# FFT and routed experts on one core: the first two half batches in a hand-written order, with the early loads on two queues

## Chip, core and metric

One core of a Trainium2 chip runs the whole kernel. The metric is the device time of one execution in microseconds (us), and the kernel before takes 1115.26 us, the median of three runs.

## What is computed

```python
X = np.fft.fft(np.fft.fft(x, axis=1), axis=2).real      # x: 8 x 2496 x 256
x = X.reshape(19968, 256)
logits = x @ w_gate                                     # 8 experts
expert_idx = np.argmax(logits, axis=1)
probs = softmax(logits); gate_w = probs[rows, expert_idx]
for e in range(8):
    mask = expert_idx == e
    h = np.maximum(x[mask] @ w1[e], 0.0)                # F = 1024
    out[mask] = gate_w[mask, None] * (h @ w2[e])
```

## The kernel before

The real part of the two transforms is folded by symmetry, so that each of the 8 batches becomes two half batches (even and odd). I number these 0 to 15: half batch 2b + par is the half `par` of batch b. A batch of x (2.6 MB) is loaded in five column slots; the first batch comes in three pieces, slots 0 and 1 (A), 2 and 3 (B), and 4 (C).

**Per half batch.** DVE folds the batch in place (`fold_w` L403, `fold_fg` L408 and L410, `fold_z` L418, `fold_h` L429 and L431). TensorE runs the *S stage* along the sequence (`s_mm` L319, matmuls L321), twice (q0, q1), and ACT and DVE evict each (`s_stage` L343, L348 to L353). The *D stage* (`along_d` L559, matmuls L567 and L568) makes five column tiles; for each ACT does three copies (L570 to L572) and DVE two (L573, L574). `route_a` (L461) makes the logits (L466), an exponent on ACT (L475), a one-hot (L483) and its bf16 copy on ACT (L487). `route_b` (L498) counts the tokens of each expert by two small matmuls (L503, L504) and a scan (L509), makes each token's slot (`di`, L521), and POOL scatters the rows into buckets in DRAM, ten scatters for a half batch (L525).

**Expert part.** After half batches 1, 3, 6, 10 and 15 a *group table* is made on DVE (`group_table` L639, `table_row` L688); its row goes to SP by DMA (L695), and SP's registers then give the addresses of the rows and weights of the groups that follow. `moe_steps` (L881) loads weights (`load_w`, L757) and rows (`load_rows`, L727), transposes on TensorE (L773), splits into a high and a low part for fp32 accuracy (ACT L775, L788, L799; DVE L776, L789, L800) and multiplies (L813 to L815, L845 to L856). Two groups belong to the first table, ten to the second.

**What sets the order.** Both parts are generators of steps; the scheduler of the language puts the instructions on the engines in an order of its own, within constraints given in the code (`issue_after`). Each engine works its list in order. Nearly all loads are on SP's DMA queue; batch 1 and the token ids (`load_rest` L256) are on POOL's. A bulk of dummy matmuls (`spin` L312, `WARM = 16, 40`) runs before the first fold is ready and while folds run. `fold_first` (L446) folds batch 0, `fold_batch` (L437) the others; `pads` (L540) writes the ends of the buckets; `load_x` (L223) loads a later batch into the buffer of the one two before. `gate_weights` (L379), `g1_fold` (L358), `g1_sums` (L367), `g1_rows` (L372) and `gate_g1` (L389) do a column that stands apart and its share of the logits. POOL also makes a bf16 copy of a triangle for the router (`trib`, L309) and puts the ids into the rows (`put_ids` L457).

## Time and profile before

| what | value |
|---|---|
| runs | 1114.73, 1115.26, 1116.75 us; median 1115.26 |
| profiled execution | 1110.62 us, span of its trace 1108.5 |
| granted clock of TensorE, mean | 0.989 |
| busy: TensorE / DVE / ACT / POOL | 97% / 74% / 54% / 33% of the span |
| bytes moved | 183.13 MB, 165 GB/s on average |

The profile is of one execution and its times are from the start of the span; 2.1 us of the 1110.62 lie around it. An engine's idle time matters only where work that ends the kernel waits for it. The trace names what ended each wait, by semaphores.

### The profile page before, as it was taken

The page shows a single profiled execution, that of the slowest core. Times are in us where ns is not written, and L with a number is a line of the kernel's source. Part 1 is how long each engine was busy: PE and PEld are TensorE (multiplying, and loading weights), DVE is VectorE, ACT ScalarE, POOL GpSimd, SP SyncE. Part 2 cuts the span into 40 slices and gives each one's busy share as a digit, 9 for nine tenths or more (in the row PEclk, how much of TensorE's full clock was granted, in tenths as well). Part 3 has the DMA queues.
Part 4 walks back from the last instruction along what each step waited for, and adds up shares of the span by engine and source line. Part 5 has one row for each costly group of instructions (what it writes and reads, how often), then busy time and mean ns, then how long its engine had stood idle before and what let it go on. Part 6 is the DMA issues. An engine that isn't in the chain of part 4 may idle for free.

```text
span 1108.5 us, 20006 instructions
## 1 busy us (share of the span) xinstructions
...
## 2 busy tenths in 40 slices
...
GB/s 352 162 197 243 141 316 196 232 238 253 231 183 82 274 202 145 138 163 144 153 190 133 151 127 156 134 159 120 157 132 161 122 54 72 149 200 46 40 68 194
DMA packets 175761, 183.13 MB, mean 165 GB/s; under 512 B 146107, under 2 KB 147037, under 8 KB 162978
## 3 DMA queue, kind: packets, MB, share of 16 engines
...
q0 software_dynamic: 16352, 45.10, 11.2%
...
## 4 chain that ended last, share of the span: by engine, by line
PE 85%; issue 6%; DMA 3%; DVE 2%; POOL 2%; ACT 1%; SPq 0%; POOLq 0%; DVEq 0%; ACTq 0%
PE psY L855 21%; PE psH L815 13%; PE psH L814 13%; PE psH L813 13%; PE psY L856 11%; PE psH L321 5%; PE psY L845 2%; PE psY L848 2%; PE psY L847 2%; PE psH L567 1%; PE psH L568 1%; DMA pack<-c_pack 1%; DMA x<-xin 1%; POOL out L869 1%; PE psH L773 1%
## 5 line engine op out<-in xcount | busy, mean ns | idle before, releaser
L855 PE MATMUL psY<-wb,hh 128*128 128x512 f32 x1104 | 401.7, 397 | 1.2 <-DVE ohf L483 0.9
L869 POOL DMA_INDIRECT out<-ys,gt x162 | 175.0, 1080 | 530.4 <-DVE ys L868 448.1
L856 PE MATMUL psY<-wb,hl 128*128 128x256 f32 x1104 | 309.0, 280 | 0.0
L813 PE MATMUL psH<-xh,wah 128*128 128x512 f32 (+1 forms) x832 | 291.0, 350 | 0.7 <-ACT xh L775 0.7
L815 PE MATMUL psH<-xh,wal 128*128 128x512 f32 (+1 forms) x832 | 288.0, 346 | 0.0
L814 PE MATMUL psH<-xl,wah 128*128 128x512 f32 (+1 forms) x832 | 287.8, 346 | 0.0
L819 DVE SCALAR_TENSOR_TENSOR hl<-psH,hh 128x512 fp32r<-128x512 f32 x324 | 222.0, 685 | 39.4 <-ACT hh L818 36.2
L855 PEld LDWEIGHTS psY<-wb,hh 128*128 128x128 f32 x1104 | 207.3, 188 | 52.5 <-issue 5.5
L789 DVE TENSOR_TENSOR wal<-w1r,wah 128x512 fp32r<-128x512 f32 x208 | 143.2, 689 | 141.9 <-ACT wah L788 141.3
L788 ACT CAST wah<-w1r 128x512 fp32r<-128x512 f32 x208 | 129.1, 621 | 203.7 <-PE psH L814 198.6
L818 ACT ACTIVATE hh<-psH 128x512 fp32r<-128x512 f32 x324 | 192.9, 595 | 53.7 <-PE psH L815 53.5
L525 POOL DMA_INDIRECT bucket<-rb,di x160 | 175.3, 1096 | 129.6 <-issue 78.5
L856 PEld LDWEIGHTS psY<-wb,hl 128*128 128x128 f32 x1104 | 208.2, 189 | 9.0
L813 PEld LDWEIGHTS psH<-xh,wah 128*128 128x128 f32 x832 | 157.6, 189 | 25.3 <-issue 3.0
L815 PEld LDWEIGHTS psH<-xh,wal 128*128 128x128 f32 x832 | 157.8, 190 | 19.1
L799 ACT CAST wb<-w2r 128x512 fp32r<-128x512 f32 x208 | 129.9, 624 | 73.1 <-PE psY L856 55.7
L800 DVE TENSOR_TENSOR wb<-w2r,wb 128x512 fp32r<-128x512 f32 x208 | 142.8, 686 | 35.0 <-ACT wb L799 34.7
L814 PEld LDWEIGHTS psH<-xl,wah 128*128 128x128 f32 x832 | 158.1, 190 | 10.7
L775 ACT CAST xh<-psH 128x512 fp32r<-128x512 f32 x81 | 47.5, 587 | 47.3 <-DVE psH L769 44.7
L866 ACT ACTIVATE ys<-psY,gt 128x256 f32<-128x256 f32 x162 | 66.0, 479 | 7.7 <-PE psY L848 4.6
L776 DVE TENSOR_TENSOR xl<-psH,xh 128x512 fp32r<-128x512 f32 x81 | 55.6, 687 | 17.7 <-ACT xh L775 16.1
L321 PE MATMUL psH<-cs,x 64*128 64x313 f32 (+3 forms) x280 | 66.1, 439 | 0.0
...
## 6 DMA issues: line engine op xcount, KB each, us to landing
...
```

Of the source, the lines that this page charges most:

```text
L525: ins = nc.gpsimd.indirect_dma_start(out=bucket[:, :], out_offset=IndirectOffsetOnAxis(ap=di[:, n : n + 1].bitcast(U32), axis=0), in_=rb[: ...
L789: nc.vector.tensor_sub(lo, src, hi.bitcast(F32))
L799: nc.scalar.copy(wb[:, :, 0], src)
L800: nc.vector.tensor_sub(wb[:, :, 1], src, wb[:, :, 0].bitcast(F32))
L813: nc.tensor.matmul(o, lhsT=wh[:, c], rhs=xh[:, k, :], start=(k == 0), stop=False)
L814: nc.tensor.matmul(o, lhsT=wh[:, c], rhs=xl[:, k, :], start=False, stop=False)
L815: nc.tensor.matmul(o, lhsT=wl[:, c], rhs=xh[:, k, :], start=False, stop=(k == 1))
L818: nc.scalar.activation(hh, hp, AF.Relu)
L819: nc.vector.scalar_tensor_tensor(out=hl, in0=hp, scalar=0.0, in1=hh.bitcast(F32), op0=ALU.max, op1=ALU.subtract)
L855: nc.tensor.matmul(y, lhsT=hh[:, c], rhs=wide_w, start=(first and q == 0), stop=end, skip_group_check=True)
L856: nc.tensor.matmul(y[:, 0:D], lhsT=hl[:, c], rhs=wb[:, f, 0], start=False, stop=end, skip_group_check=True)
L869: ins = nc.gpsimd.indirect_dma_start(out=out, out_offset=IndirectOffsetOnAxis(ap=gt[:, a, 1:2].bitcast(U32), axis=0), in_=ys, in_offset=No ...
```

## The change

- The early loads go to two queues, SP's and ACT's: batch 0 in three slots, then tables, ids and batch 1 on SP; the column part, the gate weights, the first sine and cosine table and the pieces of the constant pack on ACT. POOL issues none of them. The two small casts of POOL go to ACT.
- `fold_first` is gone. The new `start()` writes the first two half batches out by hand, under a manual schedule for TensorE, DVE and ACT: it folds slot by slot, with the halving fold per pair of slots (`fold_h` with `ns`), and puts the S stage of half batch 0 in pieces between the slots (`fill` in `s_mm`). `s_stage` is split, so that matmuls and eviction can stand apart.
- The dummy matmuls are 14 at the start and then groups of four, each tied to a fold.
- The folds of batch 1 are woven into the D stage and the routing of half batch 1, one per step; batch 2 is loaded directly after the pads.
- In `moe_steps`, the second weight load of the first group stands ahead of the load of its rows.

```diff
-WARM = 16, 40
+WARM = 14
...
-    x0 = ff.tile([P, 4, 5, 256], F32, name="x")
-    xs_of[0] = x0
-    def load_x0(sl):
-        nc.sync.dma_start(out=x0[:, :, sl[0] : sl[1]], in_=i["xin"][0][:, :, sl[0] : sl[1]])
-
-    load_x0(slots[0])
-    nc.sync.dma_start(out=xg, in_=i["xg"])
-    g0, g1 = int(ends[1]), int(ends[3])
-    for t, n in ((wg, "wg"), (wgl, "wgl"), (cdl, "c_cdl")):
-        nc.sync.dma_start(out=t, in_=i[n])
-    nc.sync.dma_start(out=pack[:, g0:g1], in_=i["c_pack"][:, g0:g1])
-    nc.sync.dma_start(out=cs0[:, 0], in_=i["c_cs0"][:, 0])
-    for sl in slots[1:]:
-        load_x0(sl)
-    for a, b in ((0, g0), (g1, int(ends[-1]))):
-        nc.sync.dma_start(out=pack[:, a:b], in_=i["c_pack"][:, a:b])
-    sines = nc.sync.dma_start(out=cs0[:, 1], in_=i["c_cs0"][:, 1])
+
+    def load_slots(b, sl):
+        if b not in xs_of:
+            xs_of[b] = ff.tile([P, 4, 5, 256], F32, name="x")
+        return nc.sync.dma_start(out=xs_of[b][:, :, sl[0] : sl[1]], in_=i["xin"][b][:, :, sl[0] : sl[1]])
+
+    A, Bp, Cp = slots
+    g0, g1, gN = int(ends[1]), int(ends[3]), int(ends[-1])
+    for t, n in ((xg, "xg"), (wg, "wg"), (wgl, "wgl"), (cdl, "c_cdl")):
+        nc.scalar.dma_start(out=t, in_=i[n])
+    nc.scalar.dma_start(out=cs0[:, 0], in_=i["c_cs0"][:, 0])
+    for a, b in ((g0, g1), (0, g0), (g1, gN)):
+        nc.scalar.dma_start(out=pack[:, a:b], in_=i["c_pack"][:, a:b])
+    for sl in slots:
+        load_slots(0, sl)
+    nc.sync.dma_start(out=cs0[:, 1], in_=i["c_cs0"][:, 1])
     for g in range(2):
         nc.sync.dma_start(out=cs1[:, g], in_=i["c_cs1"][:, g])
+    nc.sync.dma_start(out=ids.rearrange("p b n -> p (b n)"), in_=i["c_ids"])
+    for sl in slots:
+        ch["x1"] = load_slots(1, sl)
 
     def wait_for(ins, other, reason):
         tc.add_manual_dep(ins.ins, other.ins.name, mybir.DependencyInfo(mybir.DependencyClass.Sync, mybir.DependencyReason.DATA), reason=reason)
-
-    def load_rest():
...
-        for n, (o, a) in enumerate(parts):
-            ch["x1"] = nc.gpsimd.dma_start(out=o, in_=a)
...
-    nc.gpsimd.tensor_add(wsum, wg[:, 0:E], wg[:, E : 2 * E])
-    nc.gpsimd.tensor_sub(wdif, wg[:, 0:E], wg[:, E : 2 * E])
-    load_rest()
-    nc.gpsimd.tensor_copy(trib, tri)
-    nc.gpsimd.tensor_copy(tacc[:, 2:3], io[:, 2:3])
-
-    def spin(n):
+
+    def spin(n, gate=None):
 
         wp = ps.tile([P, 512], F32, name="psH", bufs=4)
         for q in range(n):
-            nc.tensor.matmul(wp, lhsT=warm[:, 0:P], rhs=warm, start=True, stop=True)
-
-
-    def s_mm(pe, po, z, zs, g, m):
+            ins = nc.tensor.matmul(wp, lhsT=warm[:, 0:P], rhs=warm, start=True, stop=True)
+            if gate is not None and q == 0:
+                wait_for(ins, gate, "no earlier than this fold")
+
+    def s_mm(pe, po, z, zs, g, m, fill=None):
 
         mm = lambda *a, **k: ch.update(pe=nc.tensor.matmul(*a, **k).ins)
         half = slice(0, 64), slice(64, 128)
@@ -330,28 +315,44 @@
             return
         c = cs0[:, g // 2]
         dif, add = z[:, 0:4:2], zs
+        ranges = list(zip((slice(0, M2), slice(M2, M)), (add, dif) if g else (dif, add)))
         lead = None
-        for k, a in zip((slice(0, M2), slice(M2, M)), (add, dif) if g else (dif, add)):
+        if fill:
+            for n, o in enumerate((pe, po)):
+                for q, (k, a) in enumerate(ranges):
+                    mm(o[0:m, k], lhsT=a[:, n, :], rhs=c[:, n, k], start=q == 0, stop=False, skip_group_check=True)
+                fill[n]()
+        for k, a in () if fill else ranges:
             with tc.issue_after(lead) if lead is not None else nullcontext():
                 for n, o in enumerate((pe, po)):
                     mm(o[0:m, k], lhsT=a[:, n, :], rhs=c[:, n, k], start=lead is None, stop=False, skip_group_check=True)
             lead = ch["pe"]
-        with tc.issue_after(lead):
+        with tc.issue_after(ch["pe"]):
             for r, o in zip(half, (pe, po)):
                 mm(o[0:m, 0:M], lhsT=z[r, 4, :], rhs=c[r, 2], start=False, stop=True, skip_group_check=True)
 
-    def s_stage(dst, z, zs, g, m):
-
-        pe, po = bank("S"), bank("S")
-        s_mm(pe, po, z, zs, g, m)
...
-        spin(WARM[0])
-        gate_weights()
-        g1_fold()
-        g1 = g1_sums(0)
-        spin(WARM[1])
-        yield from fold_first()
-        for u in range(AHEAD_IDS):
-            early_rows[u] = ff.tile([P, NK, BW], F32, name="rb", bufs=RBB)
-            put_ids(early_rows[u], *units[u])
-        along_s(0, 0)
-        along_s(0, 1)
-        ready = ch["ev"]
-        g1_rows(0, g1)
-        gate_g1(0)
-        yield from fold_z(0, 1)
-        yield from along_d(0)
-        yield from route(0)
-        along_s(1, 0)
-        along_s(1, 1)
-        g1 = g1_sums(1)
-        g1_rows(1, g1)
-        gate_g1(1)
-        yield from along_d(1)
-        yield from route(1)
-        with tc.issue_after(ready):
-            yield from fold_batch(1)
+        def run(g):
+            for _ in g:
+                pass
+
+        def weave(g, fill):
+            for _ in g:
+                next(fill, None)
+
+        def start():
+            spin(WARM)
+            g1_fold()
+            nc.gpsimd.tensor_add(wsum, wg[:, 0:E], wg[:, E : 2 * E])
+            nc.gpsimd.tensor_sub(wdif, wg[:, 0:E], wg[:, E : 2 * E])
+
+            def slot(sl, n):
+                run(fold_w(0, sl))
+                spin(4, ch["w"])
+                run(fold_fg(0, sl))
+                if n < 2:
+                    spin(4, ch["w"])
+                run(fold_z(0, 0, sl, (0,)))
+                if n < 2:
+                    run(fold_h(0, (0, 1), (n, n + 1)))
+
+            slot(slots[0], 0)
+            g1 = ff.tile([P, NKK], F32, name="pc")
+            b1 = bank("S"), bank("S")
+            s_mm(*b1, gz[:, 0], gzs, 0, B)
+            e1 = s_half(b1[0], B)
+
+            def second():
+                slot(slots[1], 1)
+                gate_weights()
+
+            def third():
+                slot(slots[2], 2)
+
+            pc = along_s_mm(0, 0, (second, third))
+            nc.scalar.copy(trib, tri)
+            nc.scalar.copy(tacc[:, 2:3], io[:, 2:3])
+            run(fold_z(0, 0, ALL, (1,)))
+            spin(4, ch["w"])
+            run(fold_h(0, (1, 2)))
+            s_evict(g1, *b1, 0, B, e1)
+            pc()
+            qc = along_s_mm(0, 1)
+            run(fold_z(0, 1, ALL, (0,)))
+            qc()
+            g1_rows(0, g1)
+            gate_g1(0)
+            run(fold_z(0, 1, ALL, (1,)))
+            for u in range(AHEAD_IDS):
+                early_rows[u] = ff.tile([P, NK, BW], F32, name="rb", bufs=RBB)
+                put_ids(early_rows[u], *units[u])
+            run(along_d(0))
+            pc = along_s_mm(1, 0)
+            st, rb = {}, cols.pop(0)
+            run(route_a(0, 0, rb, st))
+            rb0 = route_b(0, 0, rb, st)
+            next(rb0)
+            qc = along_s_mm(1, 1)
+            run(rb0)
+            pc()
+            qc()
+            g1 = g1_sums(1)
+            g1_rows(1, g1)
+            gate_g1(1)
+            fb = fold_batch(1)
+            weave(along_d(1), fb)
+            weave(route(1), fb)
+            return fb
+
+        with tc.manual_schedule(engines={mybir.EngineType.PE, mybir.EngineType.DVE, mybir.EngineType.Activation}):
+            fb = start()
         pads()
-        ch["done"] = 2 if SEGS[0][0] == 2 else 0
+        load_x(2)
+        ch["done"] = 2
+        yield
+        yield from fb
         late = None
         for u, (b, par) in enumerate(units):
             if u < 2:
                 continue
-            if par == 0 and b + 1 < B:
+            if par == 0 and 1 < b < B - 1:
                 load_x(b + 1)
             along_s(u, 0)
             yield
@@ -886,11 +939,9 @@
         if g0 == 0 or g0 >= SURE + 2:
             w_regs(g0)
             load_w(g0, w1r, "w1")
+            load_w(g0, w2r, "w2")
         if g0 == 0:
             load_rows(g0)
-        if g0 == 0 or g0 >= SURE + 2:
-            load_w(g0, w2r, "w2")
-        if g0 == 0:
             yield g0
         for part in range(2):
             xpose(g0, part)
```

The scheduler's order moves with it at three places. The names end in a tile's number; `x_117` and `x_94` are batch 1, `x_585` and `x_561` batch 2, `x_1007` batch 3.

**ACT, around the routing of half batch 2** (L467 to L507 before, L457 to L497 after). Before:

```order
L467 COPY rb_250<-rb_250 128x5x127
L348 COPY ec_744<-psH_736 128x313
L475 ACTIVATE ex_755<-ls_753 128x80
L490 ACTIVATE sm_765<-sm_765,eps_104 128x10
L487 CAST ohb_763<-ohf_761 128x80
L507 COPY sb_772<-psH_769 128x8x10
L788 CAST wah_887<-w1r0_135 128x512
L788 CAST wah_921<-w1r0_135 128x512
```

and of the changed kernel:

```order
L841 CAST wah_838<-w1r0_121 128x512
L337 COPY ec_724<-psH_716 128x313
L841 CAST wah_872<-w1r0_121 128x512
L457 COPY rb_265<-rb_265 128x5x127
L852 CAST wb_1044<-w2r0_123 128x2x256
L852 CAST wb_1082<-w2r0_123 128x2x256
L465 ACTIVATE ex_735<-ls_733 128x80
L480 ACTIVATE sm_745<-sm_745,eps_109 128x10
L477 CAST ohb_743<-ohf_741 128x80
L497 COPY sb_752<-psH_749 128x8x10
```

Of the first group's weights the casts of w1 (`wah`) and w2 (`wb`) moved from behind this routing to among its steps, and the first stands ahead of the whole of it.

**DVE, around the D stage and logits of half batch 1** (`rb`, `lg`). Before:

```order
L573 TENSOR_TENSOR rb_248<-pl_476,psH_473 128x136
L574 TENSOR_TENSOR rb_248<-pl_476,psH_473 128x136
L410 TENSOR_TENSOR x_117<-x_117 128x2x128
L573 TENSOR_TENSOR rb_248<-pl_485,psH_482 128x136
L574 TENSOR_TENSOR rb_248<-pl_485,psH_482 128x136
L418 TENSOR_TENSOR x_117<-x_117 128x5x128
L466 TENSOR_TENSOR lg_491<-rb_248,gg_114 128x80
L418 TENSOR_TENSOR x_117<-x_117 128x5x128
L470 TENSOR_REDUCE mx_494<-lg_491 128x10
L429 TENSOR_TENSOR zs_574<-x_117 128x512
L473 TENSOR_TENSOR ls_496<-lg_491,mx_494 128x80
L431 TENSOR_TENSOR x_117<-x_117 128x2x2x128
```

and of the changed kernel:

```order
L575 TENSOR_TENSOR rb_263<-pl_458,psH_455 128x136
L576 TENSOR_TENSOR rb_263<-pl_458,psH_455 128x136
L404 TENSOR_TENSOR x_94<-x_94 128x2x256
L575 TENSOR_TENSOR rb_263<-pl_468,psH_465 128x136
L576 TENSOR_TENSOR rb_263<-pl_468,psH_465 128x136
L404 TENSOR_TENSOR x_94<-x_94 128x2x256
L456 TENSOR_TENSOR lg_475<-rb_263,gg_119 128x80
L404 TENSOR_TENSOR x_561<-x_561 128x2x256
L460 TENSOR_REDUCE mx_478<-lg_475 128x10
L409 TENSOR_TENSOR x_94<-x_94 128x2x128
L463 TENSOR_TENSOR ls_481<-lg_475,mx_478 128x80
L404 TENSOR_TENSOR x_561<-x_561 128x2x256
```

A fold (L404) of batch 1 stands behind each pair of evictions, and folds of batch 2 behind the logits, where folds of a later kind of batch 1 stood.

**DVE, the routing of half batch 3** (from the reciprocal to `di`). Before:

```order
L492 RECIPROCAL rb_847<-sm_977 128x5x2
L509 SCALAR_TENSOR_TENSOR sc_988<-pack_72,sb_985 128x88
L515 TENSOR_TENSOR rp_990<-psH_982,sc_988 128x80
L644 TENSOR_TENSOR nn_1153<-sc_988,pack_72 128x8
L506 COPY sb_1580<-sc_988 128x8
L516 TENSOR_TENSOR rp_990<-rp_990,ohf_973 128x80
L648 CAST ni_1155<-nn_1153 128x8
L519 TENSOR_REDUCE dst_993<-rp_990 128x10
L649 TENSOR_SCALAR ni_1155<-ni_1155 128x8
L521 TENSOR_TENSOR di_995<-dst_993,pack_72 128x10
```

and of the changed kernel:

```order
L482 RECIPROCAL rb_894<-sm_957 128x5x2
L404 TENSOR_TENSOR x_1007<-x_1007 128x2x512
L499 SCALAR_TENSOR_TENSOR sc_968<-pack_72,sb_965 128x88
L404 TENSOR_TENSOR x_1007<-x_1007 128x2x512
L505 TENSOR_TENSOR rp_970<-psH_962,sc_968 128x80
L344 TENSOR_TENSOR pc_1010<-ec_1019,psH_1012 128x313
L506 TENSOR_TENSOR rp_970<-rp_970,ohf_953 128x80
L346 TENSOR_TENSOR pc_1010<-ec_1019,psH_1012 128x312
L509 TENSOR_REDUCE dst_973<-rp_970 128x10
L697 TENSOR_TENSOR nn_1133<-sc_968,pack_72 128x8
L496 COPY sb_1560<-sc_968 128x8
L511 TENSOR_TENSOR di_975<-dst_973,pack_72 128x10
```

Folds of batch 3 and the first eviction of the S stage of half batch 4 (`pc`) moved ahead of the last steps of this routing; row `di` is further behind, and the steps on the second table (`ni`) went behind it.

## Rows read from the trace of the kernel before

**Rows 1.** The waits of TensorE from 89.9 us to the end: who waited for whom, us in total, times, the longest.

```profile
PE psY L855 <- DVE ohf L483: 0.9, 1, 0.9
PE psY L855 <- DVE ys L868: 0.2, 1, 0.2
```

**Rows 2.** Five stretches: length; busy time and instructions of PE, PEld, DVE, ACT, POOL; granted clock of TensorE; mean busy share of the 16 DMA engines; GB/s.

```profile
2.00:18.80 16.80, 11.41 (x44) 4.83 (x43) 4.16 (x14) 0.44 (x2) 7.34 (x15) 0.90 1.00 357
41.00:47.50 6.50, 4.93 (x32) 3.20 (x31) 6.17 (x24) 2.38 (x14) 2.42 (x3) 1.00 0.96 392
70.50:73.50 3.00, 3.00 (x8) 1.18 (x6) 2.48 (x7) 0.00 (x0) 2.20 (x2) 0.50 0.77 306
80.50:83.50 3.00, 3.00 (x16) 2.99 (x15) 1.81 (x9) 1.71 (x6) 2.39 (x3) 0.50 1.01 406
90.50:94.00 3.50, 3.50 (x14) 2.34 (x14) 2.61 (x17) 0.42 (x1) 0.98 (x1) 0.52 1.01 423
```

**Rows 3.** DVE's timeline: start and duration of an instruction or of a run of equal ones (us), line, operation, out<-in and shape, count, and in brackets the idle time before it and what ended it.

```profile
6.55 1.23 DVE L403 TENSOR_TENSOR x<-x 128x1024 f32<-128x1024 f32 x1 [5.35 <-DMA x<-xin]
...
18.77 1.22 DVE L403 TENSOR_TENSOR x<-x 128x1024 f32<-128x1024 f32 x1 [8.10 <-DMA x<-xin]
...
33.19 0.29 DVE L574 TENSOR_TENSOR rb<-pl,psH 128x136 f32<-128x136 f32 x1 [1.10 <-POOL rb L459]
...
43.35 0.15 DVE L521 TENSOR_TENSOR di<-dst,pack 128x10 int32<-128x10 f32 x1
...
45.72 0.29 DVE L573 TENSOR_TENSOR rb<-pl,psH 128x136 f32<-128x136 f32 x1
...
46.14 0.29 DVE L573 TENSOR_TENSOR rb<-pl,psH 128x136 f32<-128x136 f32 x1
...
49.19 0.23 DVE L466 TENSOR_TENSOR lg<-rb,gg 128x80 f32<-128x80 f32 x1
...
53.71 0.68 DVE L403 TENSOR_TENSOR x<-x 128x512 f32<-128x512 f32 x1
...
54.31 0.33 DVE L509 TENSOR_TENSOR_SCAN sc<-pack,sb 128x88 f32<-128x88 f32 x1
...
57.13 0.16 DVE L521 TENSOR_TENSOR di<-dst,pack 128x10 int32<-128x10 f32 x1
...
58.75 0.42 DVE L408 TENSOR_TENSOR x<-x 128x256 f32<-128x256 f32 x1
...
59.08 0.17 DVE L660 TENSOR_TENSOR_SCAN end<-onef,left 128x8 f32<-128x8 f32 x1
...
91.95 0.17 DVE L521 TENSOR_TENSOR di<-dst,pack 128x10 int32<-128x10 f32 x1 [0.17 <-DVE ni L649]
...
93.58 0.48 DVE L349 TENSOR_TENSOR pc<-ec,psH 128x313 f32<-128x313 f32 x1 [0.48 <-ACT ec L348]
```

**Rows 4.** The issues on SP's DMA queue, with the same columns.

```profile
39.22 0.81 SPq L228 DMA_DIRECT2D x<-xin  x2
...
62.85 0.92 SPq L695 DMA_DIRECT2D row<-tab  x1
...
67.25 0.36 SPq L757 DMA_DIRECT2D w1r<-w  x1
...
108.85 0.35 SPq L727 DMA_DIRECT2D xr<-bucket  x1
```

**Rows 5.** ACT's timeline, with the same columns.

```profile
68.58 0.26 ACT L487 CAST ohb<-ohf 128x80 bf16<-128x80 f32 x1 [0.32 <-DVE ohf L483]
...
73.54 1.14 ACT L788 CAST wah<-w1r 128x512 fp32r<-128x512 f32 x2 [4.16 <-DMA w1r<-w]
...
81.79 0.62 ACT L799 CAST wb<-w2r 128x512 fp32r<-128x512 f32 x1 [1.48 <-DMA w2r<-w]
```

**Rows 6.** TensorE's timeline, with the same columns; a row may join matmuls that run on behind each other.

```profile
12.30 1.20 PE L321 MATMUL psY<-cs,gz 128*8 128x156 f32 x4 [5.39 <-DMA cs<-c_cs]
...
15.62 0.39 PE L381 MATMUL psH<-wsum,pack 128*128 128x8 f32 x2
...
16.89 8.81 PE L316 MATMUL psH<-rb 128*128 128x512 bf16 x39
...
25.53 0.69 PE L321 MATMUL psY<-cs,x 128*128 128x156 f32 x4
...
29.81 0.97 PE L567 MATMUL psH<-pack,pc 128*128 128x137 f32 x6
...
68.89 0.20 PE L503 MATMUL psH<-ohb,trib 128*128 128x80 bf16 x1 [2.62 <-ACT ohb L487]
...
68.99 4.71 PE L321 MATMUL psH<-cs,x 128*128 128x313 f32 x12
...
78.55 0.66 PE L773 MATMUL psH<-pack,xr 128*128 128x128 f32 x4 [2.02 <-DMA xr<-bucket]
...
89.87 0.20 PE L503 MATMUL psH<-ohb,trib 128*128 128x80 bf16 x1 [3.16 <-DMA x<-xin]
...
112.21 0.60 PE L773 MATMUL psH<-pack,xr 128*128 128x128 f32 x4
```

**Rows 7.** POOL's timeline: the first and the last of the ten scatters of half batch 3.

```profile
92.89 0.98 POOL L525 DMA_INDIRECT bucket<-rb,di  x1 [4.78 <-DVE sta L662]
...
106.05 0.98 POOL L525 DMA_INDIRECT bucket<-rb,di  x1 [0.30 <-issue]
```

51 lines of the change are left out of this document (26 added, 25 removed).

## The prediction

> **What bounds the kernel now.** Read the waits of TensorE first [rows 1]: from 89.9 us to the end it waits once 0.9 us and once 0.2 us in over a thousand. What follows the router matmul of half batch 3 (L503 at 89.87 us, called T here) is a full TensorE, and the change alters none of that work. So it can act in two ways only: T comes sooner or later, or a new stall opens behind T. Before T the path changes hands, which the timelines show in order. The first 19 us belong to the transfers: a DMA share of 1.00 [rows 2], while DVE folds slot A at 6.55 and then waits 8.1 us for slot B [rows 3]. Then DVE and TensorE make half batches 0 and 1, and DVE the first group table, whose row leaves at 62.85 [rows 4]; the weights are asked for at 67.25 and land 6.3 us later, at 73.54 [rows 4, 5]. The transpose of the first gathered rows is at 78.55, and T is 11.3 us behind it [rows 6]. I follow that chain with the changed order. The sum is made against the profiled execution, 1110.62 us; the median of the three runs shown, 1115.26, is 4.64 above it, and the sum's difference is laid on the median. About 0.2% (2.2 us) is what a measurement of this kernel can tell from no change.
>
> **The front gains.** Batch 1 (2.6 MB) and the ids leave POOL's queue and stand behind the tables on SP. Ahead of slot B are then slots A and B (2.1 MB) and at most the 1.2 MB of tables: 3.3 MB at 357 GB/s is 9.2 us, and with a start at 2 us slot B is there at about 11.2 instead of 18.77 [rows 2, 3]. Slot A I put at 7.0, near its 6.55, with its first fold of 1.23 over at 8.2. From there TensorE has its hand-written list: 24 warming matmuls at 8.81/39 = 0.23 us (5.4), the 12 passes for column sums (3.3, 12.30 to 15.62), the gate weights (1.27, 15.62 to 16.89), and the two S stages of half batch 0 (25.53 to 29.81, 4.3): 14.3 us, so 22.5, and I take 23.3 since the first has a slow part where TensorE waits for slot C, against 29.81 [rows 6]. The folds of B and C (8 of DVE's steps, 4.5 us from 11.2) lie beside it. Moving the two casts from POOL to ACT costs nothing on the path: ACT is idle there, and POOL's 6 us cast had held the ids until 33.19, a 1.1 us wait that goes [rows 3].
>
> D(0) and route(0) took 29.81 to 43.35 with five folds of batch 1 and the S(1) evictions between. The folds (3.0) and evictions (1.6) now stand behind, the 1.1 us wait is gone, so about 7.8: the slots of half batch 0 at 31.1, its first scatter at 32. S(1) and its column sums then take TensorE to 35.4, and the first D(1) eviction is at about 37.5 instead of 45.72 [rows 3]: **8.2 us gained** here.
>
> **Then DVE gives it back.** The five folds of batch 1 are now woven into D(1): 5 × (0.41 + 0.60) = 5.1, logits of half batch 1 at 42.7 (49.19 before). Into route(1) come five 512-wide folds (0.60 each) of batch 2 and six 256-wide ones (0.33) of batch 1, with 15 small steps of 0.15 (a 0.23 row overlaps the next): 7.3, so its slots are at 50.1 (57.13). The table takes 5.7 us before; now nine 256-wide folds (3.0), four 640-wide (0.73 by their width, 2.9), two 512-wide (1.2) and some 20 small steps at about 0.1 (2.2) stand in it: 9.3. The row leaves at 59.5 [rows 3, 4]. **Of 8.2 us, 3.3 are left.** Batch 2 must have landed by 43 for this: it is asked for when S(1) has read batch 0, some 6 us sooner than 39.22, and takes up to 8 us; I take it as just in time, and one or two us late at worst.
>
> **Weights before routing on ACT.** First weights are asked for 4.4 us after the row [rows 4], at 63.9, and the second 0.5 behind it, since its load moved ahead of the row gather. The first alone took 6.3, so 70.2; the second's 1.05 MB adds 2.7 at 392 to 357 GB/s: 72.4, bounds 71.5 and 74. This decides more than it looks. In the old order the one-hot cast of half batch 2 was at 68.58, ahead of the weight casts at 73.54 and 81.79 [rows 5]. In the new one, two casts of each weight stand ahead of route(2)'s steps on ACT. So the router matmul of half batch 2 waits for the second weight: 72.4 + 1.2 of casts + 1.9 for exponent, sum, one-hot and their hand-overs = 75.5, against 68.89. S(3) behind it took 4.71 at a granted clock of 0.50, the 1.2 GHz level, after a 2.6 us pause; the pause is now longer, so 4.7 again, and the transpose is at 80.1 (78.55 before). From there to T were 11.3 us; the second weight is there already, which ends a wait of 1.48 us for it on ACT, most of which was on the path: 10.2, bounds 9.5 and 11.3. **T at 90.3, so +0.4**: the gain of the front is spent [rows 2, 5, 6].
>
> *What the page says of it.* The 6.3 us of the first weight were measured beside the scatters of half batch 1; ten scatters take 13 to 14 us [rows 7], so those now end at about 64 to 65, when the loads begin. The Trainium skill ("DMA: Bandwidth & Descriptors", section "Queues, rings and completion order") states that each DMA engine takes turns between the queues that have work, a packet from each. By that rule both weights would have the engines to themselves and land at 71.5; the sum would be 0.9 less. No run here shows the loads alone.
>
> **A new stall behind T.** The slots of half batch 3 were there 2.1 us after T. Now two 1024-wide folds of batch 3 (1.2 each) and the S(4) eviction (two of 0.4 to 0.5, which itself could not start before T + 3.7) are ordered among its steps: T + 4.9 to T + 5.7 [rows 3, 6]. Ten scatters follow, 0.94 later and 13.2 long (92.89 to 106.05), then the next gather is asked for 2.8 later (108.85), with 2.25 for its bytes [rows 4, 7]: T + 24.1 to T + 24.9. TensorE comes to the transpose of those rows at T + 22.3 (112.21), and waited there for nothing before [rows 1, 6]. So it now waits 1.8 to 2.6, and I take 2.3; bounds 0 (if its order has a us of work more, or the folds start before T) and 4 (if batch 3 lands after T; its load is now behind the second pair of weights).
>
> **Sum.** +0.4 and +2.3 = +2.7 us: 1113.3 against the profiled 1110.62, or **1118.0** for the median. Its own range is 1116 to 1120, from bounds of T (89 to 91.5) and of the stall.
>
> **Rivals.**
> 1. *No change, about 1115.3.* The stall is short, or the second weight lands at 71.5 and T comes 1 to 2 us sooner, so that both cancel. For it: DVE's late folds are 0.60 us each and the order of two of them decides the stall; the bounds above reach zero. Chance 0.30.
> 2. *Faster: the clock stays up.* Place: S(3) and the first gemm. In the old trace 70.5 to 73.5, 80.5 to 83.5 and 90.5 to 94 ran at 0.50 to 0.52 [rows 2]. If the earlier front leaves TensorE without the pauses ahead of them, half of S(3)'s 4.7 and of the 6.5 us of the other two comes back: 1118.0 − 5.6 = 1112.4. It decides when the pause ahead of S(3) is under a us. Against it: the pause grows by my chain, and 2.6 us of it were enough for 0.50 in the old trace. Chance 0.10.
> 3. *Faster: weights early.* If the table's row leaves by 57.5 (its folds are drawn from batch 1, which might be ready sooner) and the second weight lands by 69.4, T is 87.3, 2.6 sooner than now; with a stall of no more than 0.3 that is 1113.0 or better. The old path to T could take it: route(2) was ready at 68.58. Chance 0.12.
> 4. *Slower still: the front itself waits.* Batch 2 is late for the folds woven into route(1), and each us of that goes through table, row and weights to T; with 2 us and a batch 3 that lands after T, 1121. Chance 0.10.
>
> **How the numbers follow.** Forecast 0.38, no change 0.30, faster 0.22, slower still 0.10. So slower by over 0.2%: 0.48; within: 0.30; faster: 0.22. The likeliest is 1118.0. The range leaves out half of the faster cases and few of the slow ones: 1112.5 to 1122.
>
> **What would show it.** Right: the first scatter at about 32; the table's row at 59 to 61; the second weight ahead of the router matmul of half batch 2, which is at 74 to 77, with the wait on ACT's cast from the second weight; T at 88.5 to 92; and TensorE waiting 1 to 4 us for the gather at its third group. Wrong: that router matmul before 71, T before 88, or no wait at the third group. If the front's scatter comes after 36, the step on early loads has failed; if the row leaves after 62, the woven folds cost more than their widths.

## The result: slower by 1.4%, and the profile after

| what | before | after |
|---|---|---|
| median, on one chip | 1116.14 us (5 runs, 1114.73 to 1116.75) | 1130.90 us (5 runs, 1127.32 to 1135.92) |
| ratio after / before | | 1.0138, interval 1.0107 to 1.0169 |
| profiled execution, span of its trace | 1110.62, 1108.5 us | 1135.92, 1134.1 us |
| granted clock, mean | 0.989 | 0.975 |

The changed kernel is 14.8 us slower; 2.7 had been forecast. The two profiled executions lie further apart, 25.6 us in span, because that of before is shorter than all five timed runs of its kernel and that of after the longest of its five. In these two traces 16.3 us are there when the last scatter is issued (1118.31 against 1101.99), and 9.3 lie behind it: POOL's last scatter in after, and a stretch behind it with the columns of [rows 2]:

```profile
1118.31 0.98 POOL L922 DMA_INDIRECT out<-ys,gt  x1 [0.30 <-DVEq L1030]
```

```profile
1123.00:1134.00 11.00, 0.00 (x0) 0.00 (x0) 0.00 (x0) 0.00 (x0) 0.00 (x0) 0.50 0.00 0
```

For the last 11 us no engine is busy and no DMA engine moves anything. From the last scatter's issue to the end it is 15.8 us here and 6.5 in before, behind the same last work. I call this the **tail**. The busy columns leave out the instructions of an engine's queue, such as drains and semaphore steps, and the difference between the two tails lies in two of these, both POOL's. First in before, then in after (count, then shortest/median/longest in ns, then the first and the last start in us):

```profile
L979 POOLq INC_SWDGE_SEM  x1: 542/542/542, 1105.6 to 1105.6; - x1
L999 POOLq DRAIN  x3: 46/103/1536, 1106.2 to 1108.3; - x3
```

```profile
L1030 POOLq INC_SWDGE_SEM  x1: 2382/2382/2382, 1121.9 to 1121.9; - x1
L1050 POOLq DRAIN  x3: 40/107/9050, 1124.3 to 1133.9; - x3
```

In after POOL's long drain starts at 1124.3 and takes 9.05 us instead of 1.54, and the step ahead of it 2.38 instead of 0.54; together that is 9.35 us more, while the other engines have reached their last instructions by 1125.0 and wait. In the traces that follow these two durations are constant for a kernel, to the nanosecond, so the tail is 9.4 of the 14.8 us, and 5.4 are left for all the rest. The forecast had no such term.

TensorE after T first (T is the router matmul of half batch 3, line 493 now). Its waits from there to the end; who waited for whom, us in total, times, longest:

```profile
PE psH L826 <- DMA xr<-bucket: 3.7, 1, 3.7
PE psH L493 <- ACT ohb L477: 3.0, 1, 3.0
...
```

The two rows left out are 0.9 and 0.2 us, those of [rows 1]. The second here is the wait that ends in T itself. The first is new: the third group's rows, 3.7 us late. Behind it TensorE is full again, so between the two ends of the chain the forecast's two ways are the only two: T moved, and one stall opened behind it. TensorE's timeline of after, the same columns as [rows 6]:

```profile
13.76 0.53 PE L306 MATMUL psY<-cs,x 128*128 128x156 f32 x2 [1.72 <-DVE x L432]
...
14.90 3.22 PE L300 MATMUL psH<-rb 128*128 128x512 bf16 x8 [0.34 <-DVE x L404]
...
28.16 0.50 PE L569 MATMUL psH<-pack,pc 128*128 128x137 f32 x2
...
83.86 0.23 PE L493 MATMUL psH<-ohb,trib 128*128 128x80 bf16 x1 [7.29 <-ACT ohb L477]
...
83.96 4.71 PE L306 MATMUL psH<-cs,x 128*128 128x313 f32 x12
88.59 0.66 PE L826 MATMUL psH<-pack,xr 128*128 128x128 f32 x4
...
99.30 0.20 PE L493 MATMUL psH<-ohb,trib 128*128 128x80 bf16 x1 [3.03 <-ACT ohb L477]
```

The first D stage starts 1.65 us before that of [rows 6], at 28.16; the router matmul of half batch 2 15.0 us behind its old place, the first transpose 10.0, and T 9.4. DVE's timeline of after, the columns of [rows 3]:

```profile
6.61 1.23 DVE L404 TENSOR_TENSOR x<-x 128x1024 f32<-128x1024 f32 x1 [2.00 <-DMA x<-xin]
...
12.55 0.17 DVE L724 SCALAR_TENSOR_TENSOR off<-fprev,pack 128x8 f32<-128x8 f32 x1 [3.39 <-DMA pack<-c_pack]
12.63 0.42 DVE L419 TENSOR_TENSOR x<-x 128x256 f32<-128x256 f32 x1
...
13.62 1.22 DVE L404 TENSOR_TENSOR x<-x 128x1024 f32<-128x1024 f32 x1
...
36.90 0.17 DVE L511 TENSOR_TENSOR di<-dst,pack 128x10 int32<-128x10 f32 x1
...
44.09 0.30 DVE L575 TENSOR_TENSOR rb<-pl,psH 128x136 f32<-128x136 f32 x1 [0.53 <-ACT rb L574]
...
56.48 0.16 DVE L511 TENSOR_TENSOR di<-dst,pack 128x10 int32<-128x10 f32 x1
...
101.22 1.23 DVE L404 TENSOR_TENSOR x<-x 128x1024 f32<-128x1024 f32 x1 [1.87 <-DMA x<-xin]
102.62 1.20 DVE L404 TENSOR_TENSOR x<-x 128x1024 f32<-128x1024 f32 x1
```

The row at 12.55 is the one to see. It is no fold: it is a step of the first group table (`off`, line 724), which needs nothing of the batch, only a piece of the constant pack. The scheduler placed it among the first folds, and DVE, which works its list in order, stood 3.39 us for that piece with slot A half folded. In the kernel before the same step stood behind the folds and waited for nothing:

```profile
27.12 0.26 DVE L671 SCALAR_TENSOR_TENSOR off<-fprev,pack 128x8 f32<-128x8 f32 x1
```

Slot B (13.62) then had no wait of its own, against 8.1 us in [rows 3].

SP's queue and ACT in after, the columns of [rows 4, 5]:

```profile
65.99 0.94 SPq L748 DMA_DIRECT2D row<-tab  x1
70.36 0.37 SPq L810 DMA_DIRECT2D w1r<-w  x1
71.01 0.34 SPq L810 DMA_DIRECT2D w2r<-w  x1
...
122.99 0.36 SPq L780 DMA_DIRECT2D xr<-bucket  x1
```

```profile
76.44 0.62 ACT L841 CAST wah<-w1r 128x512 fp32r<-128x512 f32 x1 [2.44 <-DMA w1r<-w]
...
80.99 1.14 ACT L852 CAST wb<-w2r 128x512 fp32r<-128x512 f32 x2 [1.43 <-DMA w2r<-w]
...
83.56 0.26 ACT L477 CAST ohb<-ohf 128x80 bf16<-128x80 f32 x1 [0.59 <-DVE ohf L473]
```

The one-hot cast of half batch 2, at 68.58 ahead of the weight casts in [rows 5], is now behind both and waits for the second weight. Stretches of after, the columns of [rows 2]:

```profile
16.50:20.00 3.50, 3.50 (x13) 2.62 (x11) 3.33 (x9) 0.05 (x1) 1.01 (x2) 0.50 1.02 392
20.00:24.00 4.00, 4.00 (x12) 1.89 (x12) 1.40 (x4) 0.54 (x5) 0.00 (x0) 0.50 1.05 381
...
70.50:76.50 6.00, 5.72 (x26) 3.55 (x26) 4.34 (x14) 2.32 (x16) 1.84 (x2) 1.00 0.86 277
76.50:81.00 4.50, 0.08 (x1) 0.10 (x1) 3.26 (x8) 2.14 (x5) 0.00 (x0) 0.94 0.45 184
...
124.00:130.00 6.00, 4.16 (x20) 4.19 (x21) 1.49 (x3) 1.16 (x3) 0.00 (x0) 0.57 0.34 97
130.00:140.00 10.00, 10.00 (x66) 8.39 (x66) 8.65 (x22) 6.07 (x16) 0.20 (x1) 0.92 0.09 28
```

From 16.5 to 24 TensorE had work without a gap and a granted clock of 0.50, the lower of its two levels (1.2 GHz). Right after the new stall it is low again, 0.57, then 0.92, where the kernel before had 1.00 from 120 to 140.

### The profile page after: what moved, and what is told of

Its sections match the earlier page's. It is cut to its first block, busy times and chain, and to the rows that moved or that the text cites. A ratio compares the mean times of both kernels' runs of the same rounds, so it can differ in the third digit from the quotient of the medians.

```text
span 1134.1 us, 19961 instructions
## 1 busy us (share of the span) xinstructions
PE 1074.4 (95%) x6188; PEld 914.6 (81%) x6188; DVE 825.0 (73%) x1821; ACT 602.2 (53%) x1368; POOL 356.2 (31%) x345
## 4 chain that ended last, share of the span: by engine, by line
PE 77%; issue 11%; DMA 4%; DVE 3%; POOL 2%; ACT 1%; SPq 0%; POOLq 0%; ACTq 0%; DVEq 0%
PE psY L908 19%; PE psH L867 11%; PE psH L868 11%; PE psH L866 11%; PE psY L909 10%; PE psH L306 5%; PE psY L898 2%; PE psY L900 2%; PE psY L901 2%; POOL out L922 2%; DMA x<-xin 1%; PE psH L570 1%; PE psH L569 1%; PE psY L306 1%; DMA w2r<-w 1%
## 5 line engine op out<-in xcount | busy, mean ns | idle before, releaser
L867 PEld LDWEIGHTS psH<-xl,wah 128*128 128x128 f32 x832 | 158.4, 190 | 10.7
```

The lines of the kernel that those rows point to most:

```text
L867: nc.tensor.matmul(o, lhsT=wh[:, c], rhs=xl[:, k, :], start=False, stop=False)
```

## Experiments

The theory after these traces: the loss is made in four places, (a) the wait of `off` among the first folds, (b) the weight casts ahead of the routing of half batch 2 on ACT, (c) the folds of batch 3 ahead of the slots of half batch 3 on DVE, and (d) the woven folds of batch 1. The rival for (b) was the order of the loads on SP (second weight ahead of the row gather), and for (a) TensorE's clock alone. The tail was taken for a matter of the execution until fifteen traces had it; the last three kernels are on it.

The kernels e1 to e15 ran on chips where the kernel before takes about 1200 us, e16 to e18 on one where it takes 1114.37; each ratio is to the kernel before on the same chip. Marks of two kernels can come from different chips: e1 to e8 ran on one, e9 on a second, e10 to e12 on a third, e13 to e15 on a fourth. The marks of the profiled executions (us; "third gather" is the issue of the third group's rows, "tail" from the last scatter's issue to the end of the span):

| kernel | first D stage | table row | router matmul, half batch 2 | T | third gather | last scatter | tail | ratio [95%] |
|---|---|---|---|---|---|---|---|---|
| before, first chip | 29.81 | 62.85 | 68.89 | 89.87 | 108.85 | 1101.99 | 6.5 | 1 |
| after, first chip | 28.16 | 65.99 | 83.86 | 99.30 | 122.99 | 1118.31 | 15.8 | 1.0138 [1.0107, 1.0169] |
| e9_before | 29.62 | 64.75 | 76.78 | 95.44 | 116.61 | 1179.56 | 6.5 | 1 |
| e5_same | 28.49 | 66.34 | 82.50 | 103.92 | 131.01 | 1193.56 | 16.0 | 1.0101 [1.0066, 1.0136] |
| e15_same_again | 23.90 | 61.59 | 77.90 | 99.22 | 129.22 | 1194.06 | 15.9 | 1.0094 [1.0057, 1.0131] |
| e1_pack_early | 25.74 | 63.59 | 81.22 | 102.57 | 130.87 | 1193.59 | 15.8 | 1.0101 [1.0029, 1.0172] |
| e2_w2_back | 28.18 | 65.86 | 85.41 | 106.84 | 133.85 | 1194.22 | 16.0 | 1.0122 [1.0069, 1.0176] |
| e3_no_weave | 23.95 | 62.67 | 79.27 | 102.21 | 123.70 | 1186.14 | 16.0 | 1.0065 [1.0027, 1.0104] |
| e4_route_first | 23.70 | 61.38 | 76.65 | 100.27 | 120.92 | 1191.67 | 15.9 | 1.0044 [1.0011, 1.0077] |
| e6_off_late | 21.62 | 61.28 | 77.73 | 99.11 | 126.26 | 1190.80 | 16.1 | 1.0102 [1.0050, 1.0153] |
| e7_rf_off | 21.76 | 60.90 | 74.71 | 97.16 | 118.99 | 1189.17 | 15.8 | 1.0064 [1.0029, 1.0099] |
| e8_nw_off | 21.68 | 58.86 | 72.10 | 93.28 | 115.84 | 1177.17 | 16.0 | 0.9996 [0.9967, 1.0026] |
| e14_nw_off_again | 21.73 | 60.19 | 73.83 | 96.37 | 119.73 | 1183.31 | 15.8 | 1.0008 [0.9980, 1.0037] |
| e10_x3_after | 23.72 | 61.58 | 78.84 | 100.21 | 123.95 | 1189.18 | 15.9 | 1.0081 [1.0028, 1.0135] |
| e11_nw_off_w2b | 22.18 | 61.26 | 74.34 | 96.97 | 119.51 | 1186.35 | 15.9 | 1.0029 [0.9987, 1.0070] |
| e12_early_warm | 23.16 | 56.22 | 71.68 | 90.23 | 111.28 | 1181.29 | 15.9 | 1.0038 [0.9990, 1.0086] |
| e13_early_warm_again | 23.92 | 56.92 | 70.14 | 90.86 | 110.29 | 1185.62 | 16.0 | 1.0048 [1.0017, 1.0079] |
| e16_one_act_load | 32.18 | 64.56 | 70.61 | 92.48 | 111.59 | 1105.86 | 6.5 | 0.9998 [0.9985, 1.0011] |
| e17_nw_off_sp | 24.01 | 60.78 | 68.26 | 90.73 | 111.55 | 1105.42 | 16.0 | 1.0091 [1.0067, 1.0115] |
| e18_same_sp | 24.50 | 62.16 | 78.53 | 94.31 | 116.01 | 1111.28 | 15.9 | 1.0147 [1.0126, 1.0168] |

### e5_same, e9_before, e15_same_again: the two kernels unaltered on these chips

> The changed kernel once more, unaltered, for a second trace of it on the chip that the next three run on. My theory by now (the same front ran at 1.2 GHz from 15 to 26 us in one trace and at 2.4 GHz in another, so that its first D stage is at 28.2 or at 23.7): the D stage starts at one of these two; the row leaves 21.5 to 22.5 us behind the first eviction of half batch 1, the router matmul of half batch 2 about 3 us behind the second weight's landing, and TensorE waits 2 to 5 us for the third group's rows, whatever the front does. The ratio to the kernel before is 1.010 to 1.017. Rival (the first trace was an outlier and the loss lies elsewhere): the row leaves before 62 and the ratio is under 1.006.

> The kernel before, unaltered, for a trace on the same chip as the experiments. My theory (on this chip each engine now and then stands some us with nothing to wait for, in every kernel): the first D stage is at 29 to 31 us and the table's row leaves at 62 to 65, as in the first trace, since these pauses are rare so early; the router matmul of half batch 3 is at 90 to 98, and pauses of that kind are named in its waits as well, so that they are no effect of the change. Rival (the pauses come with the changed code): its waits name none.

> The changed kernel, unaltered, once more beside these. My theory: the first D stage at 23.7 or 28.3, the third group's gather at 125 to 133, a ratio of 1.008 to 1.015. Rival (on one chip with the others it is no slower than they are): within 0.004 of their ratios.

The change costs 1.0101 and 1.0094 here, a little less than on the first chip, and the kernel before has the same order of marks as there, with pauses of its own between them (an engine stands still and the trace names no releaser). Two traces of the unaltered change differ in the front: the first D stage at 28.49 in one and at 23.90 in the other. In both DVE waits for `off`, 3.5 and 3.4 us. The same stretch of e15_same_again, to be laid beside after's 16.5 to 24, columns as before:

```profile
16.50:20.00 3.50, 3.45 (x19) 2.36 (x18) 3.33 (x9) 0.59 (x5) 1.01 (x2) 1.00 1.02 394
20.00:24.00 4.00, 4.00 (x27) 2.57 (x26) 3.06 (x7) 0.78 (x2) 0.20 (x1) 1.00 1.05 381
```

The same order, the same pause of 1.7 us ahead (1.73 at 13.91 us here, 1.72 at 13.76 in after), and twice the clock: in 20 to 24 us 27 matmuls instead of 12. So the clock, not the order, made the 4.6 us between the two front ends.

### e1_pack_early: the piece of the pack first on ACT's queue

```diff
+    nc.scalar.dma_start(out=pack[:, g1:gN], in_=i["c_pack"][:, g1:gN])
     nc.scalar.dma_start(out=cs0[:, 0], in_=i["c_cs0"][:, 0])
-    for a, b in ((g0, g1), (0, g0), (g1, gN)):
+    for a, b in ((g0, g1), (0, g0)):
```

> The changed kernel with one load moved: the last piece of the constant pack goes first of the large ones on ACT's queue. My theory (the front lost its gain because DVE stood 3.4 us at a table step, L724, that needs this piece, and TensorE then paused and ran its first stages at the 1.2 GHz level): that wait is gone, the first D stage starts at 24 to 25.5 us instead of 28.16, the first scatter at 34 to 35 instead of 38.03, the table's row leaves at 62 to 63.5 instead of 65.99, and the median is 3 to 4 us below the changed kernel's 1130.9. Rival (DVE's woven folds and the late second weight set the end whatever the front does): the row leaves within 1 us of 65.99 and the time stays at 1130 or above.

DVE's timeline of this kernel:

```profile
8.93 0.17 DVE L725 SCALAR_TENSOR_TENSOR off<-fprev,pack 128x8 f32<-128x8 f32 x1 [4.24 <-DMA pack<-c_pack]
9.01 1.22 DVE L405 TENSOR_TENSOR x<-x 128x1024 f32<-128x1024 f32 x1
```

The edit missed: with the load earlier, the scheduler put `off` ahead of the very first fold, and the wait moved from the fourth place to the first. It is 1.0101, as without the edit. To take the wait away, the step has to move, not the load.

### e2_w2_back: the second weight load behind the row gather again

```diff
             load_w(g0, w1r, "w1")
-            load_w(g0, w2r, "w2")
         if g0 == 0:
             load_rows(g0)
+        if g0 == 0 or g0 >= SURE + 2:
+            load_w(g0, w2r, "w2")
+        if g0 == 0:
             yield g0
```

> The changed kernel with the second weight's load put back behind the row gather. Rival (the load order alone costs the time, since the second weight delays the last scatter and the gather): the gather is issued at 75 to 76 instead of 80.59, the router matmul of half batch 2 comes 3 us or more sooner than 83.86, and the median is 1126 or below. My theory (the casts stand ahead of the routing on ACT, so that the weight is only awaited later): the second weight lands at 82 to 83, that router matmul is at 85 to 86, and the median is 1130 to 1134.

1.0122, with the router matmul of half batch 2 at 85.41 and everything behind it later, not earlier: its casts still stand ahead of the routing, and the cast of that weight now starts at 83.57. The order of the loads is not where the loss is; the rival for (b) falls.

### e3_no_weave: no folds woven into the D stage and routing

```diff
-            fb = fold_batch(1)
-            weave(along_d(1), fb)
-            weave(route(1), fb)
-            return fb
+            run(along_d(1))
+            run(route(1))
+            return fold_batch(1)
```

> The changed kernel without the folds of batch 1 woven by hand into the D stage and routing of half batch 1; the scheduler places them, which also puts the routing of half batch 2 ahead of the weight casts on ACT. My theory (woven folds cost DVE 4.8 us between that D stage and the table's row, and the weights before the routing cost the rest): the row leaves at 60.5 to 63 instead of 65.99, the router matmul of half batch 2 is at 70 to 74 instead of 83.86, that of half batch 3 at 89 to 92 instead of 99.30, and the median is 1116 to 1121. Rival (the early load of batch 2 and the second weight collide with the scatters, which this leaves as it is): the row leaves where it does now and the time stays above 1127.

1.0065. The third gather is 5.5 us earlier than in e15_same_again, with nearly the same front (23.95 against 23.90). But the row is 1.1 us later, not earlier, since pauses lie between (3.0 us of DVE ahead of 50.70 among others), and the scheduler, left with other due times, also put the routing of half batch 2 ahead of the weight casts. So the run speaks for the whole, not for (d) alone.

### e4_route_first: the weight casts behind the one-hot of half batch 2

```diff
+        cast = nc.scalar.copy(ohb, ohf.rearrange("p n e -> p (n e)"))
+        if (b, par) == (1, 0):
+            ch["ohb2"] = cast.ins
...
+    def behind(g):
+        return tc.issue_after(ch["ohb2"]) if g == 0 else nullcontext()
...
+        with behind(g):
             nc.scalar.copy(hi, src)
...
+        with behind(g):
             nc.scalar.copy(wb[:, :, 0], src)
```

> The changed kernel with one edge added: on ACT the casts of the first group's weights stand behind the one-hot cast of half batch 2. Everything before that stays. My theory: the table's row leaves at 65.5 to 66.5 as now, the router matmul of half batch 2 is at 76 to 78 instead of 83.86, the first transpose at 82.5 to 84.5 instead of 88.59 (the gather then sets it), and that of half batch 3 at 93 to 95.5 instead of 99.30; the scheduler also puts the folds of batch 3 behind the slots of half batch 3, so that TensorE's wait for the third group's rows is under 1.5 us instead of 3.7. The median is 1119 to 1123. Rival (the second weight's landing sets the path in any order, since the first gemm needs it): the transpose stays at 87 or later and the median above 1127.

1.0044, about half of the loss, though the interval still touches that of e5_same. The router matmul of half batch 2 is at 76.65 and the transpose at 81.23, 1.25 and 1.46 us before those of e15_same_again with a like front. T is not earlier (100.27): ACT paused 5.18 us ahead of 97.55, and the trace names no releaser for it. The scheduler put the folds of batch 3 behind the slots as well, and these were there at T + 2.1 instead of T + 5.6; the third gather is 8.3 us earlier. So (b) and (c) are mixed here.

### e6_off_late and e7_rf_off: `off` later, alone and with the casts behind

```diff
-        vec.tensor_sub(nn, carry, ebase)
+        first = vec.tensor_sub(nn, carry, ebase).ins
...
+            with tc.issue_after(first):
-            vec.scalar_tensor_tensor(out=off, in0=fprev, scalar=float(C), in1=ebase, op0=ALU.mult, op1=ALU.add)
+                vec.scalar_tensor_tensor(out=off, in0=fprev, scalar=float(C), in1=ebase, op0=ALU.mult, op1=ALU.add)
```

e7_rf_off is this with the edit of e4_route_first.

> The changed kernel with one table step (off, L724) ordered behind the table's own first step, so that it no longer stands among the folds of slot A. My theory (this step's wait for the last piece of the pack cost the front 3.4 us on DVE, and TensorE a pause of 1.7 us): the fold behind it runs at about 9.2 us instead of 12.6, the first D stage starts at 20.5 to 22 us at 2.4 GHz, and the end comes 2 to 4 us sooner than that of the unaltered kernel on the same chip. Rival (slot B's landing sets the front): the D stage stays at 23.5 or later, and the time does not move.

> Both edits: routing of half batch 2 ahead of the weight casts on ACT, and the table step out of the folds. My theory: the first D stage at 20.5 to 22, the row at 58.5 to 60.5, the router matmul of half batch 2 at 70 to 73, that of half batch 3 at 88 to 91 and no wait over 1.5 us for the third group's rows; the ratio to the kernel before is 0.997 to 1.003, so nearly all of the loss is named. Rival (a third cost, in the woven folds or in the transfers, is as large as these two): the ratio stays at 1.006 or above.

DVE's timeline of e6_off_late in the front:

```profile
6.65 1.23 DVE L404 TENSOR_TENSOR x<-x 128x1024 f32<-128x1024 f32 x1 [1.97 <-DMA x<-xin]
...
11.49 1.23 DVE L404 TENSOR_TENSOR x<-x 128x1024 f32<-128x1024 f32 x1 [1.17 <-DMA x<-xin]
```

The wait is gone, and slot B shows its landing: 11.49, where the forecast had 11.2 and the kernel before 18.77 [rows 3]. The first D stage is at 21.62 with full clock, 2.3 us before e15_same_again's. The early loads do what was forecast. Yet the time of e6_off_late (1.0102) is not different from the unaltered change: row and third gather come 5.1 and 4.8 us earlier than in e5_same, and only 0.3 and 3.0 earlier than in e15_same_again. Taking the wait away did not pay by itself. Then e7_rf_off, same front, other casts; TensorE first in e6_off_late, then in e7_rf_off:

```profile
77.73 0.23 PE L493 MATMUL psH<-ohb,trib 128*128 128x80 bf16 x1 [5.55 <-ACT ohb L477]
83.30 0.66 PE L827 MATMUL psH<-pack,xr 128*128 128x128 f32 x4
```

```profile
74.71 0.20 PE L495 MATMUL psH<-ohb,trib 128*128 128x80 bf16 x1 [2.94 <-ACT ohb L477]
79.47 0.66 PE L829 MATMUL psH<-pack,xr 128*128 128x128 f32 x4
```

The rows of the table left at 61.28 and 60.90, so nearly all of the 3.0 us (router matmul) and 3.8 us (transpose) is the casts': (b) is real. At T only 1.95 are left, since ACT pauses 5.2 us ahead of it in e7_rf_off. The slots are there at T + 2.1 instead of T + 5.6, and the third gather is 7.3 us earlier. The time falls to 1.0064, where 0.997 to 1.003 had been expected: the rival, a third cost, stands.

### e8_nw_off, e14_nw_off_again, e11_nw_off_w2b: no weave and `off` later

The edits of e3_no_weave and e6_off_late together; e11_nw_off_w2b has that of e2_w2_back too.

> The table step out of the folds, and the folds of batch 1 not woven by hand (the scheduler then also puts the routing of half batch 2 ahead of the weight casts). My theory (the woven folds lengthen DVE's way from D stage to row by some 4 us, but most of them only change places with work that must be done ahead of half batch 2 anyway): the row leaves within 2 us of that of the kernel with both other edits, and the ratio is 0.997 to 1.003. Rival (the weave is a cost of its own): 3 us or more below that kernel.

> The changed kernel without the weave and with the table step out of the folds, once more: its ratio was 0.9996. My theory: the third group's gather at 114 to 119, a ratio of 0.997 to 1.003. Rival (the first reading was chance, the weave's folds cost nothing): the ratio at 1.005 or above.

> The table step out of the folds, no weave by hand, and the second weight's load back behind the row gather: the hand-written front and the early loads remain, with none of the costs found so far. My theory (the time follows the issue of the third group's gather): the first D stage at 21 to 22.5 us, the row at 58 to 60, that gather 1 to 5 us sooner than the 116.61 of the kernel before on such a chip, and a ratio of 0.993 to 1.001. Rival (the front's gain of 8 us reaches the end once nothing holds it): 0.990 or lower.

On these two chips the loss is gone: 0.9996 and 1.0008, both intervals with 1 in them, although the tail is the long one. (With the loads on SP, on a chip without pauses, it is 1.0091: e17_nw_off_sp below.) ACT of e8_nw_off shows the routing of half batch 2 ahead of the weight casts again, and the slots of half batch 3 are at T + 2.15:

```profile
71.79 0.26 ACT L477 CAST ohb<-ohf 128x80 bf16<-128x80 f32 x1 [0.73 <-DVE ohf L473]
71.96 0.61 ACT L841 CAST wah<-w1r 128x512 fp32r<-128x512 f32 x1
```

That third cost comes with the weave, or with the order that the scheduler makes without it: e7_rf_off has the same front, the same chip and the routing ahead of the casts too, and at 1.0064 it is some 8 us slower than e8_nw_off, the two intervals apart, as the rival of e8_nw_off had it. Only 2.0 of these us are there when the row leaves. The load order (e11_nw_off_w2b, 1.0029, with its third gather 3.7 us later than that of e8_nw_off) again buys nothing. The best of these versions equals the kernel before; none beats it.

### e10_x3_after: only the folds of batch 3 behind the slots

```diff
+        ch["di", 2 * b + par] = nc.vector.tensor_add(di, dst, inval[:, n0 : n0 + NE]).ins
...
+        with tc.issue_after(ch["di", 3]) if b == 3 else nullcontext():
             ch["w"] = nc.vector.tensor_add(x[:, 0::2, s], x[:, 0::2, s], x[:, 1::2, s])
```

> The changed kernel with one edit: the first folds of batch 3 are ordered behind the slots of half batch 3; the weight casts stay ahead of the routing of half batch 2. My theory (these folds hold the slots back, and through the scatters the third group's rows): from the router matmul of half batch 3 to its slots 2 to 2.6 us instead of 5.6 to 5.9, and to the issue of the third group's gather 20.5 to 22.5 instead of 23.7 to 27; everything ahead of that matmul as in the changed kernel; ratio to the kernel before 1.005 to 1.009, so 3 to 6 us better than the unaltered 1.0101. Rival (the scatters and transfers set the gather, not the slots): the gather stays 23.5 or more behind that matmul, and the ratio at 1.010.

DVE's slots in this kernel, then in e15_same_again, whose T is a us earlier (99.22 against 100.21):

```profile
102.36 0.17 DVE L512 TENSOR_TENSOR di<-dst,pack 128x10 int32<-128x10 f32 x1 [0.17 <-DVE ni L703]
```

```profile
99.19 1.17 DVE L404 TENSOR_TENSOR x<-x 128x1024 f32<-128x1024 f32 x1
100.53 1.20 DVE L404 TENSOR_TENSOR x<-x 128x1024 f32<-128x1024 f32 x1
104.82 0.16 DVE L511 TENSOR_TENSOR di<-dst,pack 128x10 int32<-128x10 f32 x1
```

T + 2.15 against T + 5.6, as forecast. But the edit moved more than the two folds: the eviction of the S stage of half batch 4 went behind the slots with them, and in e15_same_again it is this eviction that DVE waits for last, between the second fold and the slots:

```profile
103.58 0.48 DVE L344 TENSOR_TENSOR pc<-ec,psH 128x313 f32<-128x313 f32 x1 [1.66 <-ACT ec L337]
```

So the folds and this eviction together are the delay, and the run does not part them. The gather gains more, T + 23.7 against T + 30.0, yet it stays on the rival's side of the forecast (23.5 or more). In both kernels it leaves 4.2 us behind the second table's row (119.77 and 125.00), not behind the scatters, and ahead of the row in e15_same_again DVE pauses 3.96 us, so this gain is not the edit's alone. In time it is 1.0081, an interval that overlaps that of the unaltered change. Beside e4_route_first, with the same front and the same order of these folds, the casts still stand ahead of the routing here: 78.84 against 76.65 for the router matmul and 83.62 against 81.23 for the transpose.

### e12_early_warm, e13_early_warm_again: the early loads alone

The kernel before with the two load queues, the two casts on ACT, `off` later and `WARM = 16, 16`; no hand-written order.

> The kernel before with the early loads alone: two queues, the two casts of POOL on ACT, the table step behind the table's first step, and 16 dummy matmuls instead of 40 ahead of the folds; the scheduler's order otherwise, no hand-written front. My theory (the transfers and POOL's cast bound the front, and the hand order adds little): the first D stage at 21 to 25 us instead of 29.6, the row at 57 to 61, and a ratio of 0.992 to 1.000. Rival (the hand-written order is what makes the front short): the D stage at 27 or later and the ratio within 0.002 of 1.

> The kernel before with the early loads, the table step moved and fewer dummy matmuls, once more. My theory (the end follows the third group's gather, which came 5 us sooner): that gather at 110 to 113 us against 116.6, a ratio of 0.993 to 0.999. Rival (later pauses or the tail take it back): the ratio stays at 1.000 or above.

The table's row left 8 us earlier than in e9_before (on another chip), T was 5 us and the third gather 5 to 6 us earlier, and yet the time was 1.0038 and 1.0048. With the tail it adds up: 1.0038 and 1.0048 are 4.6 and 5.8 us, and less 9.4 they are gains of 4.8 and 3.6, near to what the third gather gained, as far as the intervals (up to 1.0086 and 1.0079) tell. On that reading the earlier front reached the end, and the tail took more than it gave. This kernel has no hand-written order, so the tail does not come from that.

### e16_one_act_load, e17_nw_off_sp, e18_same_sp: what makes the tail

The theory: a DMA queue more, ACT's. All traces with early loads on it have the long tail. e16_one_act_load is the kernel before with one load there:

```diff
-    nc.sync.dma_start(out=xg, in_=i["xg"])
+    nc.scalar.dma_start(out=xg, in_=i["xg"])
```

e17_nw_off_sp (edits of e8_nw_off) and e18_same_sp (the change otherwise) have none there:

```diff
+    load_slots(0, A)
     for t, n in ((xg, "xg"), (wg, "wg"), (wgl, "wgl"), (cdl, "c_cdl")):
-        nc.scalar.dma_start(out=t, in_=i[n])
+        nc.sync.dma_start(out=t, in_=i[n])
...
-    for sl in slots:
+    for sl in (Bp, Cp):
         load_slots(0, sl)
```

> The kernel before with one small load (the column part xg) issued by ACT instead of SP, nothing else. In the two traces of the kernel before, 6.5 us lie between the last scatter's issue and the end of the span; in all fifteen of kernels with early loads on ACT's queue 15.8 to 16.1. Theory (a program that issues a DMA on ACT's queue pays some 9.4 us at its end): tail 15.8 to 16.1 and a time 9 to 10 us longer, ratio about 1.008. Rival (the tail comes from the loads that POOL no longer issues, or from the changed order): tail 6.5, ratio 1.000.

> e8_nw_off (no weave, off later) with the eight early loads of ACT's queue issued on SP's, behind slot A and ahead of slot B; ACT issues none. Theory: tail 6.5, marks as in e8_nw_off and e14_nw_off_again (first D stage 21.6 to 22.5, third gather 115 to 120), so 9.4 us less than those: ratio about 0.993. Rival (the tail belongs to the early loads themselves): tail 16, ratio 1.000.

> The change unaltered except that the eight early loads of ACT's queue are issued on SP's, behind slot A and ahead of slot B. The pack lands ahead of slot B then and the scheduler puts off behind slot A's folds, so that wait goes too. Theory: tail 6.5, and 9.4 us less than the unaltered change: ratio 1.001 to 1.003 instead of 1.0094 to 1.0101 (e6_off_late showed that the wait of off alone moved no time). Rival: tail 16 and 1.009 to 1.010.

The theory fell on all three. POOL's last scatter in e16_one_act_load (span 1112.4), then in e17_nw_off_sp (span 1121.4):

```profile
1105.86 0.98 POOL L869 DMA_INDIRECT out<-ys,gt  x1 [0.30 <-DVEq L979]
```

```profile
1105.42 0.98 POOL L923 DMA_INDIRECT out<-ys,gt  x1 [0.30 <-DVEq L1031]
```

With a load on ACT's queue the tail is 6.5 us; without any it is 16.0. But the pair shows what the tail costs as nothing else does: the same chip, the third gather at 111.59 and 111.55, the last scatter 0.4 us earlier in e17_nw_off_sp, and yet its span 9.0 us and its median 9.2 us longer (1123.05 against 1113.81). So all of e17_nw_off_sp's loss is the tail, and e18_same_sp divides the same way: its last scatter is 5.4 us behind e16_one_act_load's, its tail 9.4 longer, and its median 16.0.

What makes the tail is bounded by elimination. It is in all seventeen traces in which POOL issues no loads at the start, and in none of the three in which POOL loads the ids and batch 1. Hand order, weave and load order of the weights are not it (e12_early_warm, e3_no_weave, e2_w2_back), nor ACT's queue. What e12_early_warm shares with the others are the loads taken off POOL's queue, the two casts taken off POOL, and fewer warming matmuls (and `off` later, which e5_same has not). In all seventeen POOL's drain takes 9.05 us and the step ahead of it 2.38, in the three 1.54 and 0.54. Since the time is in POOL's own list, what POOL was given at the start, the loads and the casts, is the suspect; a kernel with one of these alone was not tried, and why POOL's closing steps should depend on them stays open.

e18_same_sp against e17_nw_off_sp is also the cleanest measure of (b), (c) and (d) together, with no pauses between and the `off` wait in neither: router matmul of half batch 2 10.3 us later, T 3.6, third gather 4.5, last scatter 5.9, ratio 1.0147 against 1.0091.

## Why the prediction was wrong

Slower was the likeliest of the three directions; the size was not: +14.8 where +2.7 had been forecast, outside the range. On the medians, 9.4 of the 14.8 are the tail and 5.4 the rest.

- **The step that failed is in "What bounds the kernel now": "So it can act in two ways only: T comes sooner or later, or a new stall opens behind T."** There was a third way, behind the last scatter, where the forecast's views end: the waits of TensorE say nothing of it, and the 6.5 us there were taken as part of the unchanged work. They became 15.9: POOL's last long drain 9.05 us instead of 1.54, the step ahead of it 2.38 instead of 0.54. In e16_one_act_load and e17_nw_off_sp the chain up to the last scatter is the same to 0.4 us and the times are 9.2 apart. With this term the forecast of 1118.0 would have been 1127.4.
- **Then "The front gains"**, its "22.5, and I take 23.3". Up to the last scatter, the chain of the forecast beside that of after's trace (first chip):

| step | forecast | measured | excess |
|---|---|---|---|
| first D stage | 23.3 | 28.16 | +4.9 |
| from there to the first D(1) eviction | 14.2 | 15.9 | +1.7 |
| to the table's row | 22.0 | 21.9 | −0.1 |
| to the first weight's issue | 4.4 | 4.4 | 0 |
| to the second weight in use | 8.5 | 10.6 | +2.1 |
| to the router matmul of half batch 2 | 3.1 | 2.9 | −0.2 |
| to the first transpose | 4.6 | 4.7 | +0.1 |
| to T | 10.2 | 10.7 | +0.5 |
| T against before | +0.4 | +9.4 | +9.0 |
| stall at the third group | 2.3 | 3.7 | +1.4 |
| behind the stall, to the last scatter | 0 | 3.2 | +3.2 |

  The loads were in time: slot A at 6.61, slot B at 11.49 where it can be seen. But the text gave DVE nothing except folds up to there and took TensorE's list at full speed. The order on DVE has a table step among the folds that waits for a constant, and TensorE, its list interrupted, fell to 0.50. The text's own sign, "If the front's scatter comes after 36, the step on early loads has failed", fired (38.03) and named the wrong part.
- The runs split the two. Without the wait the first D stage was at 21.6 to 22.2 (e6_off_late, e7_rf_off, e8_nw_off, e14_nw_off_again, e11_nw_off_w2b). With it, 23.7 to 23.95 where the clock stayed at 1.00 (e3_no_weave, e4_route_first, e10_x3_after, e15_same_again), and 28.2 to 28.5 where it fell (after, e2_w2_back, e5_same). So the wait is worth 2 us and the clock level 4.6, the latter in some executions only; the trace of after is one of them, which may be part of why it is the longest of its five.
- **"Weights before routing on ACT" was right in mechanism.** e7_rf_off against e6_off_late prices it at 3.0 to 3.8 us. Its sum for the second weight has a slip (70.2 and 2.7 are 72.9, not 72.4), and in after the weight was in use another 1.6 us later, 2.1 in all. That excess is not a property of the order: from the first weight's issue to the second's cast were 8.5 us in the forecast and 10.6 in after, but 8.2 in e6_off_late and 8.8 to 8.9 in e5_same, e15_same_again and e18_same_sp. The scatters of half batch 1, which the forecast let end at 64 to 65, were issued until 71.67, 1.3 us behind the weight's issue, and 0.7 to 1.3 behind it in those four too, so they do not make the difference. In after the share fell to 0.45 from 76.5 to 81 with the weight still to come; why stays open. The Trainium skill ("DMA: Bandwidth & Descriptors", section "Queues, rings and completion order") has the engines take turns between the queues that have work; by the reading weighed ahead of the result, both loads alone, that gave 71.5. Here its cast came at 80.99 with scatters beside the loads, and no run shows them alone.
- **"Then DVE gives it back" was right**: 22.0 forecast from the first eviction to the row, 21.9 measured. The text's sign for it, a row later than 62, fired (65.99) and named the wrong part as well. What the weave costs against the scheduler's order was not in the sum, and how it works is not settled: without it the row left 2.0 us earlier in e8_nw_off than in e7_rf_off and the time was some 8 us shorter, but in e3_no_weave the row left 1.1 us later than in e10_x3_after, and the intervals of these two overlap.
- **"A new stall behind T" was right**: slots at T + 5.86 against 4.9 to 5.7, the stall 3.7 against 1.8 to 2.6. e10_x3_after shows that the two folds of batch 3 and the eviction make the delay, as the text had it. In after 1.87 us of it are a wait for batch 3, which landed behind T; the sum had left that to a bound and to rival 4. Missed was the time behind the stall: 4.16 busy us at 0.57 and 10 at 0.92 make, as an estimate from those two rows, 2.6 us (1.8 + 0.8) of the 3.2.
- The rival "the front itself waits" had the place and, with 2 us and batch 2 as its cause, the wrong wait; its second half, a batch 3 that lands behind T, came about. "No change" and the two faster rivals did not come about, and none of the rivals had the tail.
